# A fused three-layer kernel whose last layer transposes its softmax rows as fp32r, from copies made by DMA

## The chip, the cores and the metric

The kernel runs on one core of one Trainium2 chip. The metric is the device time of one execution in microseconds; smaller is better. The engines are TensorE (PE, with its weight loads shown apart as PEld), VectorE (DVE), ScalarE (ACT), GpSimd (POOL) and SyncE (SP), which here issues every DMA from one queue, in order.

## The reference, cut to what matters

Three layers follow each other on a batch of 8 sequences of 576 tokens and 512 channels: attention through 32 memory slots, a mixing layer over tokens and then channels, and a third layer that this case is about. That third layer runs four attention experts for every sequence, of which two count for a token:

```python
for e in range(E):                     # E = 4 experts, Hd = 64
    q = x @ wq[e]; k = x @ wk[e]; v = x @ wv[e]
    scores = scale * (q @ k.transpose(0, 2, 1))
    scores = np.where(causal, -1000000000.0, scores)
    scores = scores - scores.max(-1, keepdims=True)
    a = np.exp(scores)
    a /= a.sum(-1, keepdims=True) + 1e-09
    ye = a @ v @ wo[e]
    ...                                # out += gate weight * ye where e is among the two best
```

## The kernel before

The program has three stages on the same core: layer one with the token mixing (to about 310 us), the large channel matmuls in 512-token blocks (to about 737 us), and the last layer together with the rest of the channel mixing (from 737 us on). Only the third stage is touched. Matmul operands are kept as two fp32r parts, a high and a low one, so most products are three matmuls (`mm3`).

In the third stage a loop runs over `t` from 0 to 33; step `t` computes the scores of expert pass `t` (sequence `b = t // 4`, expert `e = t % 4`; below a pass is called n) and finishes pass `t - 1`. `scores` (line 1306) writes one 128-row block c of 128(c+1) columns: two matmuls, a mask and minimum on DVE, an exponential on ACT into `a`, one of two buffers of 1280 columns (blocks c = 0 to 3 side by side). The last 64 tokens of two experts share a block of their own: `tail_scores` into `atl`. `norm` (line 1344) works out the coefficient `cf` of each row (gate over row sum) on DVE, and scales: four multiplications on POOL for c = 0, 1, 2, 3 (line 1359), and every second pass one on ACT for `atl` (line 1355). In the next step `turn` (line 1361) transposes the scaled blocks on PE against `ident`, an fp32 identity, three 128x128 tiles for c = 2, three for c = 1 and four for c = 3 (line 1378), and splits the result out of PSUM into high and low parts for `weigh`, which multiplies them with v. `tail_turn` and line 1380 do the same with `atl`. Over the 32 passes that is 400 transposes.

Between these steps the loop fills in the channel mixing of the next sequence in halves j of 288 tokens: `load_2(j)` brings `u2[j]` (line 871, 576 KB), `split_2` makes its two parts `uh2` and `ul2` on POOL (lines 884 and 885), `mm1_2` and `mm2_2` multiply, and `mm2_2` adds to `p2[j]` (line 875) and splits the sum into `xh` and `xl` (line 1215). `u2` has two buffers, and `p2[1]` takes one of them too.

A program that lays out the kernel reorders the instructions of this stage by times of its own and fixes the order on each engine. So each engine runs a given list, and waits at an instruction until what it needs is there.

The four output matmuls of `project` end in `osb` tiles and DMAs to the output. For the last sequence, block c = 1, the two halves have tiles of their own (`oh0` and `oh1`, line 1462).

Of the kernel before, what the change touches and what calls it, by code (L numbers as in the profile page):

```python
# [9 lines left out]
F32 = mybir.dt.float32  # L10
# [15 lines left out]
def f(ap):  # L26
    return ap.bitcast(F32)
# [140 lines left out]
def fused_kernel(ctx: ExitStack, tc, q, k, v, phi, w_tok1, w_tok2, w_ch1, w_ch2,  # L168
# [693 lines left out]
        stg_ctx.close()  # L862


    c2 = None
    c2_ctx, w3_ctx = ExitStack(), ExitStack()
    u2, uh2, ul2, h2, p2 = {}, {}, {}, {}, {}

    def load_2(j):
        u2[j] = c2.tile([128, KD, SH], F32, name="u2", bufs=2)  # L870
        SP.dma_start(u2[j][:], u_d[:, SH * j:SH * j + SH].rearrange("(c p) s -> p c s", p=128))

    def load_p2(j):
        p2[j] = c2.tile([128, KD, SH], F32, name="u2", bufs=2) if j == 1 else c2.tile([128, KD, SH], F32, name="p2")
        SP.dma_start(p2[j][:], x_d[:, SH * j:SH * j + SH].rearrange("(c p) s -> p c s", p=128))

    def split_2(j, kd):
# [20 lines left out]
    with ExitStack() as sb:  # L898
# [189 lines left out]
        for i in range(NW + LAG):  # L1088
            items = [()] if i == NW else [work[i]] if work[i][0] in WIDE else [(*work[i], 0), (*work[i], 1)]
            for it in items:  # L1090
                if it:
# [10 lines left out]
                    for fc in fcs:  # L1102
                        if fc > N1 + 1:
                            next(prep, None)
                        if fc >= KM - KD:
                            load_p(n, fc - KM + KD)
                        if n == 0:
                            next(wcl, None)
                        if n == 1:
                            with tc.issue_after(latest(DVE)):  # L1110
                                for _ in range(2):
                                    next(sprep, None)
                        if n > WIDE[-1]:
                            for _ in range(7):
                                if next(wcl, 0) == 0 and c2 is None:
                                    stg_ctx.close()
                                    c2 = c2_ctx.enter_context(tc.tile_pool(name="c2", bufs=1, side="right"))
                                    load_2(0)
                                    load_2(1)
# [46 lines left out]
    with ExitStack() as sc:  # L1166
# [21 lines left out]
        smb = [wk_.tile([128, NQ], F32, name=f"sm{i}") for i in range(2)]  # L1188
        aoff = [0, 128, 384, 768]
        ab = [wk_.tile([128, 1280], F32, name=f"a{i}") for i in range(2)]  # L1190

        atl = wk_.tile([128, 640], F32, name="atl")
        POOL.memset(atl[:, S:640], 0.0)
# [150 lines left out]
        def norm(n):  # L1344

            b, e = divmod(n, E)
            w = NQ - e % 2
            cf = wk_.tile([128, NQ], F32, name="cf", bufs=2)
            DVE.tensor_scalar_add(cf[:, 0:w], smb[n % 2][:, 0:w], 1e-9)
            DVE.reciprocal(cf[:, 0:w], cf[:, 0:w])  # L1350
            DVE.tensor_mul(cf[:, 0:w], cf[:, 0:w], gt[b][:, e, 0:w])  # L1351
            a = ab[n % 2]
            for c in range(w):
                if c == NQ - 1:
                    ACT.activation(atl[:, 0:S], atl[:, 0:S], AF.Copy, scale=cf[:, c:c + 1])
                    continue
                W = 128 * c + 128
                x_ = a[:, aoff[c]:aoff[c] + W]
                POOL.tensor_mul(x_, x_, cf[:, c:c + 1].to_broadcast([128, W]))  # L1359

        def turn(n, c):

            e = n % 2
            a = ab[e]
            if n not in aA:
                aA[n] = (wk_.tile([128, 384], F32R, name="Ah"), wk_.tile([128, 384], F32R, name="Al"))
                if e == 0:
# [7 lines left out]
            p = pp.tile([128, 512], F32, name="t", bufs=2)  # L1375
            with tc.high_priority():
                for kc in range(k):
                    PE.transpose(p[:, 128 * kc:128 * kc + 128], a[:, o + 128 * kc:o + 128 * kc + 128], ident[:])  # L1378
                if c == 2 and e == 0:
                    PE.transpose(p[:, 384:512], atl[:, 512:640], ident[:])  # L1380
            if c == 1:
                split(Ah[:], Al[:], p[:, 0:384])
            else:
# [8 lines left out]
        def tail_turn(n):  # L1392

            Bh, Bl, Bt = aB[n // 2]
            p = pp.tile([128, 512], F32, name="t", bufs=2)
            with tc.high_priority():
                for kc in range(4):
                    PE.transpose(p[:, 128 * kc:128 * kc + 128], atl[:, 128 * kc:128 * kc + 128], ident[:])
            split(Bh[:, :, :, 256:320].rearrange("p e k q -> p k e q"), Bl[:, :, :, 256:320].rearrange("p e k q -> p k e q"),
                  p[:].rearrange("p (k e q) -> p k e q", k=4, e=2))  # L1400

        def weigh(n, part):
# [18 lines left out]
                ops.append((4, 256, Bt[:, e % 2, :]))  # L1421
            for i, (kc, lo, x) in enumerate(ops):
                PE.matmul(p[:, lo:w], lhsT=v_[:, kc, 0, :], rhs=x, start=(i == 0), stop=(i == len(ops) - 1))  # L1423
            t_ = wk_.tile([128, 320], F32, name="yb", bufs=2)
            ACT.activation(t_[0:64, 0:w], p[64:128, 0:w], AF.Copy)
            DVE.tensor_add(yt[o:o + 64, q0:q0 + w], p[0:64, 0:w], t_[0:64, 0:w])
            if e % 2:
# [24 lines left out]
        def project(b, c):  # L1452
            last = c == NQ - 1
            if last and b % 2 == 0:
                return
            cs = slice(0, 128) if last else slice(128 * c, 128 * c + 128)
            if b == B - 1 and c == 1:
                for i, w in enumerate((slice(0, 256), slice(256, 512))):
                    p = pp.tile([128, 512], F32, name="g", bufs=GB)[:, 0:256]
                    mm3(p, [((y[0][:, cs], y[1][:, cs]), (woh[:, pr, w], wol[:, pr, w]))  # L1460
                            for pr in range(2) for y in [yT[b, pr][1:]]], late="l")
                    o_ = late.tile([128, 256], F32, name=f"oh{i}")
                    if i:
                        DVE.tensor_copy(o_[:], p)
                    else:
                        ACT.activation(o_[:], p, AF.Copy)
                    SP.dma_start(out[b, cs, w], o_[:])
                return
            p = pp.tile([128, 512], F32, name="g", bufs=GB)
            mm3(p[:], [((y[0][:, cs], y[1][:, cs]), (woh[:, pr, :], wol[:, pr, :]))  # L1470
                       for pr in range(2) for y in [yE[b // 2, pr] if last else yT[b, pr][1:]]], late="l")
            o_ = late.tile([128, 512], F32, name="osb", bufs=2) if late else wk_.tile([128, 512], F32, name="osb", bufs=2)
            if b == B - 1 and c in (3, 0):
                DVE.tensor_copy(o_[:], p[:])
            else:
                ACT.activation(o_[:], p[:], AF.Copy)
            if last:
                SP.dma_start(out[b - 1, SM:S, :], o_[0:ST, :])
                SP.dma_start(out[b, SM:S, :], o_[ST:128, :])
            else:  # L1480
                SP.dma_start(out[b, cs, :], o_[:])
# [12 lines left out]
        for c in range(KD):  # L1494
            mm2_2(1, c)
        load_2(2)
        load_2(3)
        proj(0, 1, 1, 0, True)
        proj(0, 0, 1, 1, True)
        proj(0, 0, 0, 1, True)  # L1500
# [2 lines left out]
        for t in range(NE + 2):  # L1503
# [12 lines left out]
            if e == 0:  # L1516
# [6 lines left out]
                if b == B:  # L1523
                    held = [(project, B - 2, c) for c in range(4)]
            elif e == 1:
                if b < B:
                    fill = [(proj, b, 1, i, hf) for i, hf in KQ[2:4]]
                if 0 < b < B - 1 and b - 1 not in HELD:
                    fill += [(project, b - 1, c) for c in range(3)]
                if b == B - 1:  # L1530
# [3 lines left out]
            elif e == 2:  # L1534
# [7 lines left out]
                    fill += ([(mm2_2, 2 * b + 2, c) for c in range(KD)] + [(split_2, 2 * b + 3, kd) for kd in range(KD)] +  # L1542
                             [(mm1_2, 2 * b + 3, fc) for fc in PC] + [(load_p2, 2 * b + 3)])
                if b + 2 < B:
                    fill += [(load_2, 2 * b + 4), (load_2, 2 * b + 5)]
            elif e == 3 and not more:
                held = [(project, HELD[2], c) for c in range(1, 4)]
            elif e == 3 and more:
# [102 lines left out]
```

## Time and profile before

| what | value |
|---|---|
| median of 3 runs | 1213.23 us (1211.22 to 1215.14) |
| profiled execution | 1214.76 us, its span 1213.0 us |
| PE busy over the span | 96% |
| third stage, 737 us to the end | 476 us, PE busy 465.1 us |

The span runs from the first to the last instruction; 1.8 us of the execution's own time lie outside it. The profiled execution is 1.5 us above the median. Busy time of PE counts a matmul from its start to a modelled end, so that a busy PE is not a PE at its peak; the distance between the starts of two matmuls tells what one costs.

### The profile page before, as it was taken

Reading aid. Unit: us, or ns where it says so; the run is one execution under the profiler, and the core shown is the slowest. Engines: PE = TensorE matmul, PEld = TensorE weight load, DVE = VectorE, ACT = ScalarE, POOL = GpSimd, SP = SyncE. Lnnn points to the kernel's source line nnn. Section 1 sums busy time; section 2 is a strip of 40 time slices with the busy share of each in tenths; the row PEclk is TensorE's granted clock in tenths of the full one; section 3 lists DMA queues with packets and bytes.
Section 4 is the critical chain, followed back from the end, with each engine's and each line's share of the span. In section 5 each row is a group of like instructions: output and inputs, shape, how many; then the busy total and the mean of one; then the engine's idle time right before and its main releaser. Section 6 shows DMA issues by size and latency. Waiting matters only on the chain.

```text
span 1213.0 us, 23508 instructions
## 1 busy us (share of the span) xinstructions
PE 1165.3 (96%) x8586; PEld 1064.7 (88%) x8586; DVE 816.3 (67%) x1992; ACT 610.8 (50%) x1591; POOL 449.5 (37%) x603
## 2 busy tenths in 40 slices
PE   4899998999999999999999999999999999999998
PEld 3678887999888888889999889999999999999986
DVE  6999998665483756567566514777676767676664
ACT  3565565454442323223322213677676767677775
POOL 2774453442002012112111344545454627383331
PEclk9799999999999999999999999999999999999999
DMA  8896767532370221232123343322333333322522
GB/s 239 251 276 209 215 212 221 171 118 92 97 251 20 105 70 35 71 104 97 43 71 105 96 113 114 88 84 79 84 88 83 102 97 99 94 80 54 166 86 105
DMA packets 133780, 145.07 MB, mean 120 GB/s; under 512 B 35616, under 2 KB 101408, under 8 KB 133664
## 3 DMA queue, kind: packets, MB, share of 16 engines
q1 hardware_dynamic: 133664, 143.57, 39.2%
q8 instruction: 68, 1.11, 0.4%
q14 instruction: 48, 0.39, 0.1%
HBM read 91.10 MB, written 40.89 MB: 109 GB/s over the span
## 4 chain that ended last, share of the span: by engine, by line
PE 79%; DVE 11%; DMA 3%; issue 2%; ACT 2%; POOL 1%; SPq 0%; DVEq 0%; ACTq 0%; POOLq 0%
PE g L207 21%; PE o L207 16%; PE h L207 16%; PE y L1423 4%; PE b L207 3%; PE s L1314 3%; PE b L679 3%; PE t L1378 3%; PE s L1336 1%; DVE ul L670 1%; DVE cy L772 1%; PE g L623 1%; PE g L383 1%; PE g L624 1%; PE g L626 1%
## 5 line engine op out<-in xcount | busy, mean ns | idle before, releaser
L1359 POOL TENSOR_TENSOR a<-a,cf 128x128 f32<-128x128 f32 (+3 forms) x128 | 88.3, 723 | 68.9 <-DVE cf L1351 64.9
L207 PE MATMUL o<-hl,w2h 128*128 128x512 f32 x288 | 112.7, 391 | 0.3 <-DVE hl L931 0.3
L207 PE MATMUL o<-hh,w2l 128*128 128x512 f32 x288 | 112.3, 390 | 0.0
L207 PE MATMUL o<-hh,w2h 128*128 128x512 f32 x288 | 108.7, 392 | 0.2 <-DVE pb L1026 0.2
L930 ACT ACTIVATE hh<-m 128x256 fp32r<-128x256 f32 x96 | 38.9, 416 | 111.8 <-DVE m L1001 72.2
L1303 DVE CUSTOM_DVE_ANT_0 ssb<-s,cmask 128x128 f32<-128x128 f32 (+2 forms) x144 | 68.5, 483 | 27.3 <-PE s L1314 20.5
L1316 ACT ACTIVATE a<-ssb,nb 128x128 f32<-128x128 f32 (+3 forms) x128 | 71.3, 558 | 18.4 <-DVE nb L1303 15.1
L207 PE MATMUL h<-uh,w1h 128*128 128x512 f32 (+2 forms) x200 | 66.5, 334 | 4.7 <-ACT uh L211 4.7
L931 DVE SCALAR_TENSOR_TENSOR hl<-m,hh 128x256 fp32r<-128x256 f32 x96 | 58.2, 615 | 17.6 <-ACT hh L930 15.4
L978 POOL TENSOR_TENSOR tl<-ub,th 128x512 fp32r<-128x512 f32 x12 | 18.1, 1526 | 136.3 <-ACT th L977 136.3
L207 PE MATMUL h<-uh,w1l 128*128 128x512 f32 (+2 forms) x200 | 66.7, 334 | 0.0
L1215 POOL TENSOR_TENSOR xl<-p,xh 128x288 fp32r<-128x288 f32 x60 | 47.4, 811 | 51.8 <-ACT xh L1214 51.6
L207 PE MATMUL h<-ul,w1h 128*128 128x512 f32 (+2 forms) x200 | 66.1, 335 | 0.0
L207 PE MATMUL g<-xh,qkh 128*128 128x288 f32 x232 | 65.3, 301 | 0.0
L207 PEld LDWEIGHTS o<-hh,w2l 128*128 128x128 f32 x288 | 54.1, 188 | 11.3
L207 PE MATMUL g<-xh,qkl 128*128 128x288 f32 x232 | 63.9, 296 | 0.0
L207 PEld LDWEIGHTS o<-hh,w2h 128*128 128x128 f32 x288 | 54.0, 188 | 10.7 <-DVE pb L1026 1.0
L963 POOL TENSOR_TENSOR ub<-ub 128x512 f32<-128x512 f32 x6 | 9.8, 1628 | 144.4 <-DVE ul L214 144.4
L207 PEld LDWEIGHTS o<-hl,w2h 128*128 128x128 f32 x288 | 54.1, 188 | 10.0 <-DVE hl L931 0.6
L214 DVE TENSOR_TENSOR Bl<-t,Bh 128x512 fp32r<-128x512 f32 (+1 forms) x80 | 50.5, 633 | 14.3 <-ACT Bh L211 12.6
L923 DVE SCALAR_TENSOR_TENSOR hl<-h,hh 128x512 fp32r<-128x512 f32 x24 | 16.5, 689 | 59.9 <-ACT hh L922 59.8
L1430 POOL TENSOR_TENSOR yl<-yt,yh 128x256 fp32r<-128x256 f32 x30 | 22.2, 739 | 85.0 <-ACT yh L1429 74.9
(340 smaller groups left out, 4123.8 us busy)
## 6 DMA issues: line engine op xcount, KB each, us to landing
cst<-in_moe_w_ch_dram SPq DMA_DIRECT2D x24, 512.0 KB, 4.8
u_d<-u SPq DMA_DIRECT2D x32, 288.0 KB, 3.6
p_d<-u SPq DMA_DIRECT2D x16, 576.0 KB, 4.2
ub<-u_d SPq DMA_DIRECT2D x9, 1024.0 KB, 5.7
pb<-p_d SPq DMA_DIRECT2D x36, 256.0 KB, 4.1
x_d<-pb SPq DMA_DIRECT2D x36, 256.0 KB, 2.1
u<-u_d SPq DMA_DIRECT2D x16, 576.0 KB, 4.2
p<-x_d SPq DMA_DIRECT2D x15, 576.0 KB, 4.1
```

The source lines that it names most:

```text
L207: PE.matmul(ps, lhsT=a, rhs=b, start=start and i == 0, stop=stop and i == len(seq) - 1)
L214: DVE.tensor_sub(lo, src, f(hi))
L679: PE.matmul(h1[j, fc, "p"][:], lhsT=w[:, kd, :], rhs=x[:, kd, :], start=(part == 0 and i == 0), stop=(part == 1 and i == KD - 1))
L930: ACT.activation(hh, c, AF.Relu)
L931: DVE.scalar_tensor_tensor(hl, c, 0.0, f(hh), op0=OP.max, op1=OP.subtract)
L1215: POOL.tensor_sub(xl[b][:, c, ss], x_, f(xh[b][:, c, ss]))
L1303: DVE.tensor_tensor_reduce(out=out, in0=p, in1=mask, scale=-scale, scalar=least, op0=OP.add, op1=OP.min, accum_out=acc)
L1314: PE.matmul(p[:, 0:W], lhsT=q_[n][:, 128 * c:128 * c + 128], rhs=kk[n][:, 0:W], start=(i == 0), stop=(i == 1))
L1316: ACT.activation(a[:, aoff[c]:aoff[c] + W], s_[:, 0:W], AF.Exp, scale=-1.0, bias=nb[:, 0:1], accum_out=sm[:, c:c + 1])
L1359: POOL.tensor_mul(x_, x_, cf[:, c:c + 1].to_broadcast([128, W]))
L1378: PE.transpose(p[:, 128 * kc:128 * kc + 128], a[:, o + 128 * kc:o + 128 * kc + 128], ident[:])
L1423: PE.matmul(p[:, lo:w], lhsT=v_[:, kc, 0, :], rhs=x, start=(i == 0), stop=(i == len(ops) - 1))
```

## The change

For 31 of the 32 passes (all but the last) the scaled softmax rows are no longer transposed from `a` itself. SP copies them by DMA into `ar`, a tile of the same size that is typed fp32r, and PE transposes that against an fp32r identity `identr`, which ACT makes once. The copies are three for each pass (c = 2; c = 0 and 1 together; c = 3), and POOL multiplies in that order. The tail rows `atl` are copied to `atr` in all 16 cases. `ar` and `atr` have one buffer each. The copies add 31 x 3 + 16 = 109 DMAs, and about 25 MB, to SP's queue. To make room, `u2` goes down to one buffer (half 1 alone has a place of its own), `yb` goes down to one buffer, and the last output tiles share `osb`; `load_2` of an odd half is called three steps later than before.

```diff
     def load_2(j):
-        u2[j] = c2.tile([128, KD, SH], F32, name="u2", bufs=2)
+        u2[j] = (wk8 if j == 1 else c2).tile([128, KD, SH], F32, name="u2")
...
     def load_p2(j):
-        p2[j] = c2.tile([128, KD, SH], F32, name="u2", bufs=2) if j == 1 else c2.tile([128, KD, SH], F32, name="p2")
+        p2[j] = c2.tile([128, KD, SH], F32, name="u2" if j == 1 else "p2")
...
+        identr = wk_.tile([128, 128], F32R, name="identr")
+        ACT.activation(identr[:], ident[:], AF.Copy)
+        ar = {}
...
             a = ab[n % 2]
-            for c in range(w):
-                if c == NQ - 1:
-                    ACT.activation(atl[:, 0:S], atl[:, 0:S], AF.Copy, scale=cf[:, c:c + 1])
-                    continue
-                W = 128 * c + 128
-                x_ = a[:, aoff[c]:aoff[c] + W]
-                POOL.tensor_mul(x_, x_, cf[:, c:c + 1].to_broadcast([128, W]))
+            copied = n < NE - 1
+            ar[n] = wk_.tile([128, 1280], F32R, name="ar") if copied else a
+            if e % 2 == 0:
+                ar["t"] = wk_.tile([128, 640], F32R, name="atr")
+                ACT.activation(atl[:, 0:S], atl[:, 0:S], AF.Copy, scale=cf[:, NQ - 1:NQ])
+            for cs in ((2,), (0, 1), (3,)):
+                for c in cs:
+                    W = 128 * c + 128
+                    x_ = a[:, aoff[c]:aoff[c] + W]
+                    POOL.tensor_mul(x_, x_, cf[:, c:c + 1].to_broadcast([128, W]))
+                if copied:
+                    o = slice(aoff[cs[0]], aoff[cs[-1]] + 128 * cs[-1] + 128)
+                    SP.dma_start(f(ar[n][:, o]), a[:, o])
+                if e % 2 == 0 and cs == (2,):
+                    SP.dma_start(f(ar["t"][:]), atl[:])
...
-            a = ab[e]
+            a = ar[n]
+            idn, ty = (identr, F32R) if n < NE - 1 else (ident, F32)
...
-                    PE.transpose(p[:, 128 * kc:128 * kc + 128], a[:, o + 128 * kc:o + 128 * kc + 128], ident[:])
+                    PE.transpose(p[:, 128 * kc:128 * kc + 128].bitcast(ty), a[:, o + 128 * kc:o + 128 * kc + 128], idn[:])
...
-            t_ = wk_.tile([128, 320], F32, name="yb", bufs=2)
+            t_ = wk_.tile([128, 320], F32, name="yb")
...
             if b == B - 1 and c == 1:
+                o2 = wk_.tile([128, 512], F32, name="osb", bufs=2)
...
-                    o_ = late.tile([128, 256], F32, name=f"oh{i}")
+                    o_ = o2[:, w]
...
         load_2(2)
-        load_2(3)
...
             elif e == 1:
+                if more:
+                    fill += [(load_2, 2 * b + 3)]
...
-                    fill += [(load_2, 2 * b + 4), (load_2, 2 * b + 5)]
+                    fill += [(load_2, 2 * b + 4)]
```

The order on the engines shows three places. The first is PE where pass 28 is transposed (`t` is the PSUM tile, `s` the scores of pass 29, `g` an output projection). Before:

```order
L207 MATMUL g<-woh,yl_14879 128x512
L1314 MATMUL s<-kk,qa 128x512
L1314 MATMUL s<-kk,qb 128x512
L207 MATMUL g<-woh,yl_14883 128x512
L1378 MATMUL t<-ident,a_8610 128x128 x6
L1380 MATMUL t<-ident,atl 128x128
L207 MATMUL g<-woh,yh_14878 128x512
```

And in the change, from the same scores to the last of the same seven transposes:

```order
L1319 MATMUL s<-kk,qa 128x512
L1319 MATMUL s<-kk,qb 128x512
L1392 MATMUL t<-identr,ar 128x128 x3
L207 MATMUL g<-woh,yh_15024 128x512
...
L207 MATMUL g<-woh,yl_15029 128x512
L1394 MATMUL t<-identr,atr 128x128
L1392 MATMUL t<-identr,ar 128x128 x3
```

What stood in one run of seven is now a run of three and a run of four, with 12 projection matmuls between. Between the last tail score of pass 28 and its first transpose there were 87 matmuls with 28,064 columns, and there are now 73 with 24,696. Over the whole stage the 400 transposes stood in 93 unbroken runs, so that 307 were followed at once by another; they now stand in 107 runs, and of the 390 fp32r ones 286 are followed at once by another.

The second place is SP's queue at the start of the third stage (names that begin with `u_` are buffers of `u2` and, on line 875, of `p2[1]`). Before, `u_8774` is half 2:

```order
L1027 DMA x_d<-pb 128x512 x4
L871 DMA u_8774<-u_d 128x4x288
L875 DMA p_9208<-x_d 128x4x288
L871 DMA u_8776<-u_d 128x4x288
L871 DMA u_9381<-u_d 128x4x288
L1245 DMA qb<-qa 64x576
```

In the change half 2 is `u_8780`:

```order
L1027 DMA x_d<-pb 128x512 x4
L875 DMA p_9224<-x_d 128x4x288
L871 DMA u_8780<-u_d 128x4x288
L1250 DMA qb<-qa 64x576
L1249 DMA qa<-qb 64x576
```

The load of half 2 stood first and could go as soon as half 1 had been split; it now goes into the buffer that `p2[1]` holds, and so behind the last reader of `p2[1]`. On PE, 36 projection matmuls of 288 columns (into three tiles) now stand between the end of `mm2_2(1)` and the first matmul that reads half 2, where there were none.

The third place is the end of ACT's list, the last output tiles. Before:

```order
L1425 ACTIVATE yb<-y 64x256
L1429 ACTIVATE yh<-yt 128x256
L1476 ACTIVATE osb<-g 128x512 x2
L1466 ACTIVATE oh_15742<-g 128x256
L1646 UNCONDITIONAL_BRANCH
```

And in the change:

```order
L1439 ACTIVATE yb<-y 64x256
L1443 ACTIVATE yh<-yt 128x256
L1491 ACTIVATE osb<-g 128x512 x2
L1481 ACTIVATE osb<-g 128x256
L1662 UNCONDITIONAL_BRANCH
```

The order is the same; the last half tile is now a buffer of `osb`, which the tail block (c = 4) filled two tiles earlier.

## Rows read from the trace of the kernel before

**Rows 1.** The page's first part: busy time, share of the span and instructions.

```profile
PE 1165.3 (96%) x8586; PEld 1064.7 (88%) x8586; DVE 816.3 (67%) x1992; ACT 610.8 (50%) x1591; POOL 449.5 (37%) x603
```

**Rows 2.** Third stage: us, busy PE, PEld, DVE, ACT, POOL, granted clock, DMA share, GB/s.

```profile
737.00:1213.00 476.00, 465.12 (x3396) 447.95 (x3396) 320.13 (x1028) 329.48 (x952) 230.21 (x354) 1.00 0.33 95
```

**Rows 3.** Groups by form, 737 us to the end: busy us, mean ns.

```profile
L1378 PE MATMUL t<-ident,a 128*128 128x128 f32 x320 | 48.8, 274 | 0.1
```

**Rows 4.** Timeline of PE, transposes of pass 28: start us, us from first start to last end.

```profile
1167.50 0.82 PE L1378 MATMUL t<-ident,a 128*128 128x128 f32 x6
1168.16 0.27 PE L1380 MATMUL t<-ident,atl 128*128 128x128 f32 x1
...
1168.50 0.39 PE L207 MATMUL g<-wol,yh 128*128 128x512 f32 x1
```

**Rows 5.** Timeline of PE, two 128-column fp32r matmuls in a row.

```profile
981.71 0.22 PE L1314 MATMUL s<-kk,qa 128*128 128x128 f32 x1
981.76 0.28 PE L1314 MATMUL s<-kk,qb 128*128 128x128 f32 x1
981.88 0.33 PE L1314 MATMUL s<-kk,qa 128*128 128x256 f32 x1
```

**Rows 6.** Plain fp32 weight loads of 128 columns (line 393), ns min/median/max.

```profile
L393 PEld LDWEIGHTS g<-ones,es x28: 186/190/338, 38.5 to 272.3; 128*128 128x128 f32 x28
```

**Rows 7.** Plain fp32 matmuls of 128 columns (line 383), ns min/median/max.

```profile
L383 PE MATMUL g<-kv,ea x640: 270/273/423, 9.9 to 271.6; 128*32 128x128 f32 x160
```

**Rows 8.** Line 439, transposes with 128 weight and 32 moving columns.

```profile
L439 PEld LDWEIGHTS t<-ident,qe x64: 132/138/221, 14.6 to 279.2; 32*128 32x128 f32 x64
L439 PE MATMUL t<-ident,qe x64: 221/222/311, 14.6 to 279.2; 32*128 32x32 f32 x64
```

**Rows 9.** Timeline of PE, four of these.

```profile
187.74 0.43 PE L439 MATMUL t<-ident,qe 32*128 32x32 f32 x4
```

**Rows 10.** POOL's scaling by form, 737 us to the end.

```profile
L1359 POOL TENSOR_TENSOR a<-a,cf 128x384 f32<-128x384 f32 x32 | 26.6, 830 | 0.0
...
L1359 POOL TENSOR_TENSOR a<-a,cf 128x256 f32<-128x256 f32 x32 | 19.7, 616 | 0.0
...
L1359 POOL TENSOR_TENSOR a<-a,cf 128x128 f32<-128x128 f32 x32 | 12.9, 402 | 68.9 <-DVE cf L1351 64.9 <-ACT Bh L211 3.3
```

**Rows 11.** Timeline, pass 28: after its last tail score, and its scaling on POOL.

```profile
1154.30 0.28 PE L207 MATMUL g<-vgh,xh 128*128 128x260 f32 x1
...
1163.80 2.76 POOL L1359 TENSOR_TENSOR a<-a,cf 128x128 f32<-128x128 f32 x4 [0.61 <-DVE cf L1351]
```

**Rows 12.** DMA issues: count, KB each, median us from issue to landing.

```profile
qb<-qa SPq DMA_DIRECT2D x32, 144.0 KB, 2.4
...
yh<-y_d SPq DMA_DIRECT2D x6, 256.0 KB, 5.1
...
out_dram<-osb SPq DMA_DIRECT2D x8, 128.0 KB, 2.4
```

**Rows 13.** Timeline, start of the third stage.

```profile
747.91 0.29 PE L207 MATMUL g<-uh,w1h 128*128 128x288 f32 x1
...
748.34 0.82 DVE L1213 TENSOR_TENSOR u<-u,g 128x288 f32<-128x288 f32 x2
...
749.88 1.59 POOL L1215 TENSOR_TENSOR xl<-u,xh 128x288 fp32r<-128x288 f32 x2
...
751.50 1.12 SPq L871 DMA_DIRECT2D u<-u_d  x2
...
755.53 1.55 POOL L884 CAST uh<-u 128x288 fp32r<-128x288 f32 x4 [3.30 <-DMA u<-u_d]
```

**Rows 14.** Timeline, the end.

```profile
1208.08 0.59 SPq L1479 DMA_DIRECT2D out_dram<-osb  x1
1208.55 0.42 DVE L1464 COPY oh<-g 128x256 f32<-128x256 f32 x1
...
1209.39 0.89 SPq L1467 DMA_DIRECT2D out_dram<-oh  x2
```

More of the change, by code (lines that the diff above doesn't have):

```diff
@@ L862, in fused_kernel @@
         stg_ctx.close()
-    c2 = None
+    c2 = wk8 = None
     c2_ctx, w3_ctx = ExitStack(), ExitStack()
@@ L1116, in fused_kernel @@
                                     stg_ctx.close()
+                                    wk8 = sb.enter_context(tc.tile_pool(name="wk8", bufs=1))
                                     c2 = c2_ctx.enter_context(tc.tile_pool(name="c2", bufs=1, side="right"))
@@ L1377, in turn @@
                 for kc in range(k):
-                    PE.transpose(p[:, 128 * kc:128 * kc + 128], a[:, o + 128 * kc:o + 128 * kc + 128], ident[:])
+                    PE.transpose(p[:, 128 * kc:128 * kc + 128].bitcast(ty), a[:, o + 128 * kc:o + 128 * kc + 128], idn[:])
                 if c == 2 and e == 0:
-                    PE.transpose(p[:, 384:512], atl[:, 512:640], ident[:])
+                    PE.transpose(p[:, 384:512].bitcast(F32R), ar["t"][:, 512:640], identr[:])
             if c == 1:
@@ L1397, in tail_turn @@
                 for kc in range(4):
-                    PE.transpose(p[:, 128 * kc:128 * kc + 128], atl[:, 128 * kc:128 * kc + 128], ident[:])
+                    PE.transpose(p[:, 128 * kc:128 * kc + 128].bitcast(F32R), ar["t"][:, 128 * kc:128 * kc + 128], identr[:])
             split(Bh[:, :, :, 256:320].rearrange("p e k q -> p k e q"), Bl[:, :, :, 256:320].rearrange("p e k q -> p k e q"),
@@ L1461, in project @@
                             for pr in range(2) for y in [yT[b, pr][1:]]], late="l")
-                    o_ = late.tile([128, 256], F32, name=f"oh{i}")
+                    o_ = o2[:, w]
                     if i:
-                        DVE.tensor_copy(o_[:], p)
+                        DVE.tensor_copy(o_, p)
                     else:
-                        ACT.activation(o_[:], p, AF.Copy)
-                    SP.dma_start(out[b, cs, w], o_[:])
+                        ACT.activation(o_, p, AF.Copy)
+                    SP.dma_start(out[b, cs, w], o_)
                 return
@@ L1471, in project @@
                        for pr in range(2) for y in [yE[b // 2, pr] if last else yT[b, pr][1:]]], late="l")
-            o_ = late.tile([128, 512], F32, name="osb", bufs=2) if late else wk_.tile([128, 512], F32, name="osb", bufs=2)
+            o_ = wk_.tile([128, 512], F32, name="osb", bufs=2)
             if b == B - 1 and c in (3, 0):
@@ L1525, in fused_kernel @@
             elif e == 1:
+                if more:
+                    fill += [(load_2, 2 * b + 3)]
                 if b < B:
-                    fill = [(proj, b, 1, i, hf) for i, hf in KQ[2:4]]
+                    fill += [(proj, b, 1, i, hf) for i, hf in KQ[2:4]]
                 if 0 < b < B - 1 and b - 1 not in HELD:
```

## The prediction, written before the result was known

> **What bounds the kernel now.** I read the page's first part for the engine that is nearest to full: PE, 96% of the span [rows 1]. Then the stretch in which the change lies: in the 476 us of the third stage PE is busy 465.1 us, ACT 329, DVE 320 and POOL 230, the granted clock is 1.00 (the 2.4 GHz level) and the DMA engines are busy a third of the time [rows 2]. So the third stage is a list of PE instructions with some 11 us of gaps in 476. Whatever shortens that list shortens the kernel, as long as the others keep up; whatever makes PE wait at a point of the list lengthens it by the wait. Everything below is one or the other.
>
> **What a transpose costs now.** A group of the view by form gives 274 ns for one [rows 3], but that is a duration with its pipeline in it. The timeline gives the spacing: six transposes last 0.82 us from first start to last end, so (0.82 - 0.27) / 5 = 0.110 us lie between two starts [rows 4]; I use 109 ns, as 1168.16 - 1167.50 = 0.66 is six of them. The last of a run is followed by a plain matmul: from 1168.16 to the second matmul behind it, at 1168.50, go 0.34 us. A column of plain work costs 13.20 us / 28,064 = 0.47 ns (both numbers under 2, below), so the 512-column matmul between takes 0.24 and the last transpose 0.10 to 0.11 too.
>
> **What an fp32r transpose would cost.** No row of before shows one, so I bound it. It is a weight load of 128 columns (the softmax tile) and a pass of 128 columns (the identity).
> The pass: a plain fp32 matmul of 128 columns lasts 273 ns [rows 7], as the fp32 transpose does, while a plain fp32r one of 128 columns lasts 0.22 us and the next may start 0.05 to 0.06 us later [rows 5]. So the length of the pass goes by the type, and an fp32r pass should be spaced by about 59 ns.
> The load: a plain fp32 load of 128 columns lasts 190 ns [rows 6], a transpose's 138 ns [rows 8]: here the mode counts. Four transposes with 128 weight columns and only 32 moving ones last 0.43 us, (0.43 - 0.222) / 3 = 0.069 us apart [rows 8, 9], so loads in this mode can follow each other every 69 ns at most.
> Against this stands the plain fp32r load. Of the two 128-column matmuls in [rows 5] the second starts 0.05 us after the first, but what follows it starts 0.12 us after that: 0.17 us for the two, where two passes would take 0.12. The second waited for its weights, which came about 0.11 us after the first began. If an fp32r transpose loads like that, it is spaced by 111 ns and nothing is gained.
> I take 64 ns, between 59 and 69, because two rows say that the mode sets the load and the type the pass. The bounds are 59 and 111.
> One page of the Trainium skill speaks against it: "TensorE: Matmul & The Clock Gate", section "LDWEIGHTS (loading the stationary operand)", gives a load of P columns as P / 1.2 ns, 107 ns for 128, whatever else it is; by it the sum below would hold 286 x 2 ns = 0.6 us of gain instead of 12.9. The plain pair [rows 5] agrees with it, the four short transposes [rows 9] do not, and the rows decide.
>
> **The sum.** (1) In a run of transposes only those that are followed by another get shorter, since the last one pays for the plain load behind it (0.11 us, as above). The order of the change has 286 fp32r ones followed by another: 286 x (109 - 64) = **-12.9 us**. Bounds: 286 x 50 = -14.3, and 286 x 2 = +0.6.
>
> (2) The copies. A block's way from POOL to PE gets longer by a DMA. The nearest row is the SBUF-to-SBUF copy `qb<-qa`, 2.4 us from issue to landing [rows 12]; 2.0 is thinkable, and 5.1 as the upper end, the slowest of that size class. POOL now scales c = 2 first, which saves 0.402 + 0.616 = 1.02 us [rows 10]. So the first transpose of a pass may come 1.4 us later than now without loss. I took the distance from POOL's end to the first transpose for each pass, and corrected it by the PE work that the new order puts between the last score and that transpose. Most passes have 1.5 to 10 us left. The worst is pass 28. There PE went from 1154.30 to 1167.50, 13.20 us, through 28,064 columns [rows 4, 11]; the new order has 24,696, so 13.20 x 24,696 / 28,064 = 11.6 us, and PE is at its transpose at 1165.9. POOL started at 1163.80, so c = 2 is scaled at 1164.63 [rows 10, 11] and copied at 1167.0: PE waits **+1.1 us**, and behind it the pass's other matmuls. Three other passes with e = 0 or 2 come out within 0.6 us of nothing left; I charge **+0.5 us**. Bounds for both together: 0 and, with 4 us for a copy, about 10.
> SP pays about 0.5 us for each of 109 issues, spread over the stage, and waits in the order in which POOL works; at nothing, and if it queues, the copies come later, which is the bound just given. POOL does the same work in another order; ACT gets one activation more. `yb` with one buffer: the DVE add that frees it comes before the next ACT write in all 64 cases of the trace; at nothing.
>
> (3) `u2` with one buffer. In the steady part the next load can go when POOL has split the half before, some 10 us or more ahead of its use, and takes 4 us; hidden. If that cover were gone, it would cost up to 4 us for each of 15 halves. At the start it is not hidden. Half 2 now waits for the last reader of `p2[1]`, which is `xl` on POOL. The DVE adds end at 749.16 [rows 13], ACT's copy and POOL's subtraction (0.81 each at most) behind them, without the split that now stands between them on POOL, bring that to about 750.4. Issue to the first cast took 755.53 - 751.50 = 4.0 us [rows 13], the cast takes 0.4: half 2 is ready at 754.8. PE ended `mm2_2(1)` at 747.91 and now has 36 projections of 288 columns before it needs it, 36 x 288 x 0.47 ns = 4.9 us, at 752.8. PE waits **+2.0 us**. Bounds: 0 if other waits have made PE late by then, 3.2 if the reader is as late as now (load at 751.50).
>
> (4) The end. The last half tiles write into the `osb` buffer that the tail block filled, and so wait for its two DMAs. The second is issued at 1208.08 and lands 2.4 us later [rows 12, 14], at 1210.5; a copy out of PSUM takes 0.42 us [rows 14], so the first of the two last DMAs is issued at 1210.9 instead of 1209.39: **+1.5 us**. Bounds 1.0 and 2.0. Nothing is behind it to hide it.
>
> Together -12.9 + 1.1 + 0.5 + 2.0 + 1.5 = -7.8 us. The profiled execution took 1214.8 us, so it becomes 1207.0; it lies 1.5 us above the median, and against that I forecast **1205.4 us**.
>
> **The rivals.** *The fp32r transpose costs what the fp32 one does* (slower). Its place is the weight load: if an fp32r tile loads like the plain fp32r weights of [rows 5], the spacing is 111 ns, term 1 is +0.6 and the others stay: 1213.2 + 5.7 = 1218.9 us. It decides above 109 - 5.1 / 0.286 = 91 ns, where the gain no longer pays for the waits. For it speaks that plain loads do that in every type; against it the loads of [rows 8, 9]. The page of the Trainium skill cited above would have it so. 17%.
>
> *The copies come late in many passes.* For it: one queue carries everything, 109 DMAs more, and `yh<-y_d` needed 5.1 us when twelve were sent together [rows 12]. At 4.1 us for a copy the margins of nine passes are gone and the waits add up to some 8.5 us more: about 1214 us, no change. Against it: DMA engines are busy 0.33 [rows 2], and 25 MB more at the stage's rate bring that to about half. 12%.
>
> *The waits are smaller than I make them*, because PE arrives late for other reasons, and the transposes reach 59 ns: -14.3 + 1.5 gives 1200.4 us. Little speaks against it except the arithmetic of (2) and (3). 8%.
>
> The forecast itself has 63%, with 1202 to 1209 as its own range.
>
> **How the numbers follow.** About 0.3% is what a measurement of this kernel tells from no change: below 1209.6 is faster, above 1216.9 slower. The forecast and the third rival are faster but for a tail (0.69); the first rival is slower; the second divides between no change and slower. So 0.69, 0.13 and 0.18. The range runs from 1200 to 1218.5: it leaves out the lower half of the third rival, the upper half of the first, and copies slower than 4.5 us.
>
> **What would show it.** A run of three fp32r transposes should last about 0.22 + 2 x 0.064 = 0.35 us from first start to last end, and one's weight load 138 ns; with 0.44 us and 188 ns the first rival is right. PE's busy time in the third stage should fall from 465 to about 452. The waits of PE should name the DMA `ar<-a` at pass 28 for about 1 us and at few other places, and once, near 753, the cast of half 2 for about 2 us. At the end ACT's last copy should stand idle for a DMA of `osb`. The forecast is wrong if the transposes keep their spacing, or if waits for `ar` come back in most passes with e = 0.

## The result: slower, 1227.7 us

The change takes 1227.68 us (median of 4 runs, 1225.24 to 1228.20) against 1213.28 us before (4 runs): a ratio of 1.0115 with an interval of 1.0094 to 1.0137, or 14.4 us more where 7.8 us less was forecast.

The first part of the page and the row of the third stage answer to [rows 1, 2]:

```profile
PE 1165.0 (95%) x8586; PEld 1057.2 (86%) x8586; DVE 820.4 (67%) x1992; ACT 609.8 (50%) x1592; POOL 450.3 (37%) x603
```

```profile
737.00:1227.00 490.00, 466.61 (x3405) 442.80 (x3403) 325.31 (x1031) 329.25 (x952) 229.09 (x353) 1.00 0.46 144
```

PE is busy about as long as before, though its transposes got cheaper (below), and the stage is longer; the granted clock is 1.00 in both, the DMA share went from 0.33 to 0.46. So a gain was made and more than given back. Where, is seen in what each queue waits for. Each row names the instruction that waits, what it waits for, and how long: us in total, times, longest. First PE in the third stage, then SP (SPq is its DMA queue):

```profile
PE t L1392 <- DMA ar<-a: 3.1, 5, 1.5
PE t L207 <- DVE kk L1241: 2.0, 2, 1.6
PE s L1319 <- DVE nb L1308: 1.9, 5, 0.6
PE g L207 <- DVE p L1218: 1.5, 2, 0.9
PE y L1437 <- ACT Bh L211: 1.5, 2, 1.0
```

```profile
SPq L1250 <- ACT qa L1243: 68.1, 13, 15.6
SPq L1370 <- PE t L1392: 47.4, 13, 6.5
...
SPq L1370 <- POOL a L1367: 11.7, 21, 2.4
```

No single wait of PE is large. But SP stands 47 us, in 13 places, before a copy into `ar` (line 1370) because PE has not finished the transposes of the pass before; with all other releasers it stands 105 us before the copies of lines 1370 and 1372. These are not yet costs. Before, SP stood even longer in the third stage, about 385 us in all its waits against about 340 in the change, the largest of them being

```profile
SPq L1245 <- ACT qa L1238: 83.6, 13, 16.1
SPq L871 <- POOL ul L885: 56.4, 11, 11.5
```

SP is not short of time; it matters at which instruction of its list it stands, and what PE needs from behind it.

The view of waits counts only time in which no matmul is running by its modelled end, and so undercounts. I therefore took the starts of all PE matmuls in the third stage of each trace. A plain matmul is priced at the median distance to the next start for its column count (0.060 us for 128, 0.120 for 256 and 260, 0.133 for 288, 0.148 for 320, 0.175 for 384, 0.232 for 512), transposes at the mean distance between two in a run (leaving out the few distances that hold a wait), and the end of a run at its median. The end of a run is the time from its last transpose to the second matmul behind it, less the first one's own price. What is left is waiting; by how the medians are taken it moves by about 1 us. In us, with the experiments below:

| kernel | transpose to transpose | end of a run | transposes together | waits | last matmul to end of span |
|---|---|---|---|---|---|
| before | 307 x 0.109 | 93 x 0.112 | 43.9 | 19.5 | 4.8 |
| the change | 293 x 0.074 | 107 x 0.155 | 38.2 | 35.9 | 5.9 |
| e1, no copies, fp32 | 295 x 0.110 | 105 x 0.112 | 44.1 | 20.9 | 6.0 |
| e2, copies, fp32 | 288 x 0.110 | 112 x 0.112 | 44.1 | 36.0 | 6.1 |
| e3, no copies, fp32r | 282 x 0.073 | 118 x 0.153 | 38.6 | 19.6 | 6.3 |
| e4, three tiles, fp32r | 291 x 0.073 | 109 x 0.156 | 38.0 | 31.5 | 6.1 |
| e5, unread copies, fp32 | 297 x 0.110 | 103 x 0.112 | 44.1 | 28.4 | 5.9 |
| e7, before with fp32r | 310 x 0.076 | 90 x 0.157 | 37.8 | 19.1 | 4.8 |

The plain matmuls come to 407 to 410 us in all of these. Of the 19.5 us of waits before, the view of waits shows 6; the other 13 are scatter around the medians and the 0.1 to 0.2 us by which each wait is undercounted, and something like them is in every row. The change: -5.7 (transposes) + 16.4 (waits) + 1.2 (plain) + 1.1 (end) = +13.0 of the 13.2 us by which the span grew. No plain matmul got dearer: in the change seven more of them lie behind 737 us.

### The profile page after: what moved, and what is told of

Read it like the earlier page. It is cut to its first block, busy times and chain, and to the rows that moved or that the text cites. A ratio compares the mean times of both kernels' runs of the same rounds, so it can differ in the third digit from the quotient of the medians.

```text
span 1226.2 us, 23676 instructions
## 1 busy us (share of the span) xinstructions
PE 1165.0 (95%) x8586; PEld 1057.2 (86%) x8586; DVE 820.4 (67%) x1992; ACT 609.8 (50%) x1592; POOL 450.3 (37%) x603
## 4 chain that ended last, share of the span: by engine, by line
PE 72%; DVE 12%; DMA 7%; ACT 4%; issue 2%; POOL 2%; SPq 1%; DVEq 0%; ACTq 0%; POOLq 0%
PE g L207 18%; PE o L207 16%; PE h L207 15%; PE b L207 3%; PE y L1437 3%; PE b L679 3%; PE s L1319 2%; PE t L1392 1%; DMA qn<-in_q_dram 1%; DMA p<-x_d 1%; POOL a L1367 1%; PE g L623 1%; PE s L1341 1%; DVE ul L670 1%; PE g L624 1%
## 5 line engine op out<-in xcount | busy, mean ns | idle before, releaser
L1367 POOL TENSOR_TENSOR a<-a,cf 128x256 f32<-128x256 f32 (+3 forms) x128 | 88.0, 720 | 67.5 <-DVE cf L1356 55.3
L214 DVE TENSOR_TENSOR Bl<-t,Bh 128x512 fp32r<-128x512 f32 (+1 forms) x80 | 50.4, 633 | 19.5 <-ACT Bh L211 17.1
L207 PEld LDWEIGHTS o<-hl,w2h 128*128 128x128 f32 x288 | 54.1, 188 | 10.3 <-DVE hl L931 0.7
```

The source lines that it names most:

```text
L207: PE.matmul(ps, lhsT=a, rhs=b, start=start and i == 0, stop=stop and i == len(seq) - 1)
L214: DVE.tensor_sub(lo, src, f(hi))
```

## The experiments

Ratios are to the kernel before, measured beside each experiment (12.1 us is 1%), with their 95% intervals.

**e1, the change without its copies and without fp32r.**

```diff
-            copied = n < NE - 1
+            copied = False
...
-                ar["t"] = wk_.tile([128, 640], F32R, name="atr")
+                ar["t"] = atl
...
-                if e % 2 == 0 and cs == (2,):
-                    SP.dma_start(f(ar["t"][:]), atl[:])
...
-            idn, ty = (identr, F32R) if n < NE - 1 else (ident, F32)
+            idn, ty = ident, F32
...
```

> The change without its copies and without fp32r: the transposes read the softmax rows themselves, against the fp32 identity; one u2 buffer, one yb buffer, the shared osb and POOL's new order stay. In the trace of the change PE's waits are 18 us longer than before, and the transposes and what follows them 7.6 us shorter. Theory A (the copies make the waits: their time, SP's queue, the one buffer of ar): only the start and the end remain, some 2.4 + 1.1 us, so 1215 to 1219 us. Theory B (the smaller buffers and the new order of PE make them): the waits stay and the gain is gone, 1230 us or more.

Measured 1215.46 us, 1.0029 (1.0017 to 1.0040): 3.4 us. The smaller buffers and the new order cost no more than the start and the end. Theory B is out: the copies make the waits, directly or through the order that is laid out around them, since every kernel here has an order of its own.

**e2, the change with fp32 copies and transposes**, the tail's too.

```diff
-            ar[n] = wk_.tile([128, 1280], F32R, name="ar") if copied else a
+            ar[n] = wk_.tile([128, 1280], F32, name="ar") if copied else a
...
-            idn, ty = (identr, F32R) if n < NE - 1 else (ident, F32)
+            idn, ty = ident, F32
...
```

> The change with ar and atr typed fp32 and transposed against the fp32 identity: the copies stay, the cheaper transposes go. If the type of the transposes is worth what the trace of the change shows (293 transposes that are followed by another at 67 instead of 109 ns, less 106 times 43 ns for the plain matmul that follows a run, so 7.6 us), and all else stays: 1227.7 + 7.6 = 1235 us. If the shorter transposes only make PE wait longer for the same copies, the type is worth nothing and it stays at 1226 to 1230 us.

Measured 1230.44 us, 1.0145 (1.0128 to 1.0162). It lies between the two expectations, at the upper edge of the second. Against the change, by the two ratios, that is 0.3% (3.6 us) for the type, and the intervals overlap; the table gives 5.9 us for the transposes and equal waits. Against e1 the copies cost 1.16%, 14 us.

**e3, the change without copies, with fp32r transposes.** POOL and ACT write the rounded rows themselves.

```diff
...
-                    POOL.tensor_mul(x_, x_, cf[:, c:c + 1].to_broadcast([128, W]))
-                if copied:
-                    o = slice(aoff[cs[0]], aoff[cs[-1]] + 128 * cs[-1] + 128)
-                    SP.dma_start(f(ar[n][:, o]), a[:, o])
+                    POOL.tensor_mul(ar[n][:, aoff[c]:aoff[c] + W], x_, cf[:, c:c + 1].to_broadcast([128, W]))
```

> The change without its copies, but with fp32r transposes: POOL and ACT write the scaled rows straight into ar and atr, rounded to fp32r, so the low part of the rows is lost. One u2 buffer, one yb buffer and the shared osb stay. Theory A (the copies make the waits): the run before of this call less 7.6 us, 1207 to 1212 us. Theory B (buffers and order make them): 1222 to 1228 us, as the change.

Measured 1210.82 us, 0.9995 (0.9981 to 1.0008), inside theory A's interval. Against e1 the type is worth 0.34%, 4 us, where the table has 5.5; the waits are those of e1, 19.6 and 20.9. The copies of the change move the rows bit for bit; here they are rounded and lose their low part, as in e7, e8 and e11.

**e4, three tiles for ar.**

```diff
...
-                    SP.dma_start(f(ar[n][:, o]), a[:, o])
+                    ar[n, cs[-1]] = wk_.tile([128, o.stop - o.start], F32R, name=f"ar{cs[-1]}")
+                    SP.dma_start(f(ar[n, cs[-1]][:]), a[:, o])
...
```

> The change with three tiles (384, 384 and 512 columns) in place of the one tile ar of 1280, so that the copy of a block waits only for the transposes of that block one pass earlier, not for all ten. In the trace of the change SP waits 47 us in 13 places for the transposes before it can issue such a copy. Theory A1 (that wait, and what stands behind it on SP, makes the waits of PE): 1214 to 1219 us. Theory A2 (the time of a copy, 2.4 us, between POOL and PE makes them) or B: 1224 to 1229 us.

Measured 1220.11 us, 1.0062 (1.0050 to 1.0074), between the two expectations. The one tile costs about 0.5%, 6 us, and its interval does not meet the change's; 8 us over e3 remain (9 by the two medians).

How the one tile holds the copies up shows in the trace of the change (start us, us from first start to last end; in brackets how long the engine had stood, and for what):

```profile
833.71 5.46 POOL L1367 TENSOR_TENSOR a<-a,cf 128x384 f32<-128x384 f32 x8 [8.57 <-DVE cf L1356]
...
838.99 0.40 ACT L1321 ACTIVATE a<-ssb,nb 128x128 f32<-128x128 f32 x1 [3.66 <-DMA ar<-a]
...
843.32 0.45 PE L1392 MATMUL t<-identr,ar 128*128 128x128 f32 x4
843.85 2.31 SPq L1370 DMA_DIRECT2D ar<-a  x3
```

POOL had scaled two passes by 839.2. The three copies of the second go out at 843.85, after the last four transposes of the first (843.77), though the first blocks of `ar` had long been read. A copy holds its source too: shortly before, ACT, which must not overwrite `a` before a copy has read it, had stood for 3.66 us until a copy of the first pass had landed.

**e5, copies that nobody reads.** The kernel of e1, with copies in the three tiles of e4:

```diff
+                if n < NE - 1:
+                    o = slice(aoff[cs[0]], aoff[cs[-1]] + 128 * cs[-1] + 128)
+                    un = wk_.tile([128, o.stop - o.start], F32R, name=f"ar{cs[-1]}")
+                    SP.dma_start(f(un[:]), a[:, o])
+                if e % 2 == 0 and cs == (2,):
+                    ut = wk_.tile([128, 640], F32R, name="atr")
+                    SP.dma_start(f(ut[:]), atl[:])
```

> The kernel of e1 (fp32 transposes of the softmax rows themselves, small buffers) with the 109 copies added in three tiles and one for the tail, which nobody reads. So the copies load SP's queue and the DMA engines and hold the buffers a and atl, but are not in the way from POOL to PE. The three tiles of e4 cost 9.3 us over e3, which has no copies. Theory A3 (SP's queue: what stands behind a copy that waits for POOL comes late): most of the 9 us come back, 1221 to 1226 us. Theory A2 (the time of a copy between POOL and PE): as e1, 1214 to 1218 us.

Measured 1223.17 us, 1.0088 (1.0074 to 1.0101): 7 us over e1, as much as the read ones of e4 cost over e3 (8 us). So that PE must wait for a copy's 2.4 us (theory A2) is a matter of 1 or 2 us, about what these intervals tell; by the starts of the matmuls PE waits 1.4 us right before transposes of `ar` in e4. SP's queue in e5:

```profile
SPq L1371 <- POOL a L1367: 32.8, 43, 4.6
SPq L1450 <- ACT yeh L1457: 27.6, 3, 16.7
SPq L1374 <- ACT a L1321: 18.6, 3, 8.0
```

Lines 1371 and 1374 are the unread copies: SP still stands 84 us before them with all releasers, and all that is behind them stands too. But the copies also hold `a` and `atl`, so e5 does not show that the queue alone makes the 7 us.

**e6, e4 with the copies issued by POOL and ACT.**

```diff
-                    SP.dma_start(f(ar[n, cs[-1]][:]), a[:, o])
+                    POOL.dma_start(f(ar[n, cs[-1]][:]), a[:, o])
...
-                    SP.dma_start(f(ar["t"][:]), atl[:])
+                    ACT.dma_start(f(ar["t"][:]), atl[:])
```

> The kernel of e4 (three tiles, copies read as fp32r) with the copies of the rows issued by POOL and those of the tail by ACT, each behind its own scaling, so that SP's queue is as it was before. Theory A3 (SP's queue): near e3, 1210 to 1214 us. Theory A2 (the time of a copy): it stays near e4, 1218 to 1222 us, or is longer, since POOL now waits for the transposes of the pass before.

Measured 1259.42 us, 1.0388 (1.0374 to 1.0402). This did not test SP's queue, since it made POOL a worse one. Two groups of POOL in the third stage (busy us, mean ns, idle before and its releasers):

```profile
L1367 POOL TENSOR_TENSOR a<-a,cf 128x384 f32<-128x384 f32 (+3 forms) x128 | 87.9, 717 | 26.6 <-DVE cf L1356 24.5 <-ACT qa L1243 1.5
L1371 POOL DMA_DIRECT2D ar<-a x93 | 51.7, 557 | 46.2 <-issue 14.9 <-PE t L1397 9.9 <-PE t L1395 7.1
```

Each issue takes 0.56 us of POOL, 52 us together, and 46 us go in waits in front of them, for transposes among others, while the splits of `u2` and `p2` stand behind on POOL. The Trainium skill, "DMA: Bandwidth & Descriptors", section "Issuing engines are not separate DMA queues", says that issuing from several engines only saves the sequencer's time of issue; here that time was moved onto an engine that had work to do.

**e7, the kernel before with the type alone.** The exponentials and the scaled rows are written, rounded, as fp32r into `a` and `atl`:

```diff
-        ab = [wk_.tile([128, 1280], F32, name=f"a{i}") for i in range(2)]
+        ab = [wk_.tile([128, 1280], F32R, name=f"a{i}") for i in range(2)]
+        identr = wk_.tile([128, 128], F32R, name="identr")
+        ACT.activation(identr[:], ident[:], AF.Copy)
...
-                POOL.tensor_mul(x_, x_, cf[:, c:c + 1].to_broadcast([128, W]))
+                POOL.tensor_mul(x_, f(x_), cf[:, c:c + 1].to_broadcast([128, W]))
...
```

> The kernel before with nothing but the type of the transposes changed: the exponentials and the scaled rows are written as fp32r into the same tiles a and atl (rounded), and transposed against identr. No copies, no second tile, all buffers as before. The transposes and what follows them are worth 7.7 us by the traces (43.9 us before, 36.2 to 36.4 us with fp32r in three kernels); the start (2.4 us) and the end (1.2 us) of e3 go away too. By that sum 1204 to 1206 us. If the shorter list of PE only waits more elsewhere, 1208 to 1211 us.

Measured 1206.16 us, 0.9952 (0.9938 to 0.9967): 5.8 us faster, at the upper edge of the sum. The table's 43.9 - 37.8 = 6.1 us is that gain; the 7.7 of the expectation (and the 7.6 of e1 to e3) had taken 67 ns, the median, for the distance of two transposes, where the mean is 74 to 76.

**e8, e7 without the low parts**, which are zero there, since the rows are already rounded:

```diff
...
-                split(Bh[:, e, 0:k, q0:q0 + 128], Bl[:, e, 0:k, q0:q0 + 128],
-                      p[:, 0:128 * k].rearrange("p (k q) -> p k q", k=k))
+                ACT.activation(Bh[:, e, 0:k, q0:q0 + 128], p[:, 0:128 * k].rearrange("p (k q) -> p k q", k=k), AF.Copy)
...
-                ops = [(kc, 128 * kc, x[:, 256 * kc:256 + 128 * kc]) for x in (Ah, Al) for kc in range(2)]
+                ops = [(kc, 128 * kc, x[:, 256 * kc:256 + 128 * kc]) for x in (Ah,) for kc in range(2)]
...
```

> The kernel of e7 without the low parts Al and Bl of the transposed rows, which are zero there since the rows are already rounded to fp32r: six matmuls fewer in each of the 32 passes (two for Ah's columns, four for Bh's, of 128 to 320 columns), and three subtractions fewer on DVE. If PE is the bound there: 2 x (256 + 128) / 2 and 3 x 320 + 192 columns make 1536 columns a pass, at 0.47 ns a column 0.72 us, for 32 passes 23 us below e7, about 1182 us. If ACT or DVE or POOL bound it by then, 5 to 15 us.

Measured 1184.38 us, 0.9771 (0.9758 to 0.9785): 28 us faster than before, 22 us faster than e7. PE's busy time in the third stage falls to 434 of 445 us, and it is still the engine that bounds:

```profile
737.00:1182.40 445.40, 433.78 (x3187) 414.88 (x3186) 261.05 (x911) 323.22 (x948) 226.91 (x350) 0.99 0.34 99
```

**e9 and e10, what about an unread copy costs.** Both are e5 but for what is copied, the tail's copy likewise. e9 copies 16 columns each, behind the same waits; e10 copies whole blocks of `kk`, which is ready early.

```diff
-                    SP.dma_start(f(un[:]), a[:, o])
+                    SP.dma_start(f(un[:, 0:16]), a[:, o.stop - 16:o.stop])
...
```

```diff
-                    SP.dma_start(f(un[:]), a[:, o])
+                    SP.dma_start(f(un[:]), f(kk[n][:, 0:o.stop - o.start]))
...
```

> The kernel of e5 with its 109 unread copies at the same places of SP's queue, behind the same waits for POOL, but of 16 columns each (8 KB instead of 192 to 320 KB). e5 cost 7 us over e1. Theory A4 (SP's queue: copies that wait for POOL hold up what stands behind them): it stays near e5, 1220 to 1225 us. Theory A5 (the bytes: the other transfers get slower while the copies run): as e1, 1214 to 1217 us.

> The kernel of e5 with its 109 unread copies at nearly full size (192 and 256 KB, 288 KB for the tail), but taken from the keys kk, which are ready early, so that the copies wait for neither POOL nor ACT. Theory A4 (the waits for POOL in SP's queue): as e1, 1214 to 1217 us. Theory A5 (the bytes): near e5, 1220 to 1225 us.

Measured 1220.58 us, 1.0072 (1.0061 to 1.0084), and 1219.82 us, 1.0060 (1.0047 to 1.0073). Over e1 that is 5 us and 4 us, where e5 has 7 us. Taking away nearly all bytes leaves most of the cost, as theory A4 has it; the intervals of e9 and e5 overlap. But taking away the waits for POOL and ACT (SP stands 28 us before the copies instead of 84, and 18 of these 28 for an earlier copy into the same tile) leaves half, which A4 has not. So the waits for POOL and ACT do not make the 7 us alone, and the bytes are not shown to have a part; see below.

**e11, e7 with each transpose of the rows twice.**

```diff
-                    PE.transpose(p[:, 128 * kc:128 * kc + 128].bitcast(F32R), a[:, o + 128 * kc:o + 128 * kc + 128], identr[:])
+                    for _ in range(2):
+                        PE.transpose(p[:, 128 * kc:128 * kc + 128].bitcast(F32R), a[:, o + 128 * kc:o + 128 * kc + 128], identr[:])
```

> The kernel of e7 with each of the 320 transposes of the rows a issued twice in a row (the tail's 80 once), so that the runs get longer and the result stays. By the traces an fp32r transpose starts 60 and 65 ns behind the first two of a run, and 85 ns behind the later ones. If a weight load every 85 ns sets the pace once the loads ahead are used up: 320 x 85 ns = 27 us more than e7, 1233 us. If the pass of 60 ns set it and the 85 are waits of another kind: 19 us more, 1225 us. If each cost the 109 ns of fp32: 35 us more, 1241 us.

Measured 1231.81 us, 1.0158 (1.0145 to 1.0172). Against e7 that is 2.07%, 25 us, 78 ns for each of the 320: nearest to the pace of 85 ns, not to 60 or 109. By the starts of the matmuls the transposes take 64.8 us instead of 37.8, 84 ns for each of the 320.

## Why the prediction was wrong, point by point

The step that failed is in (2): it put the waits of SP for the copies "at nothing", and so the copies at 1.6 us, where they cost some 15. Term (1) went the right way, but was taken at more than twice its size.

**(1) The transposes, forecast -12.9 us, measured -5.7.** The direction held, the first rival (111 ns, no gain) is out. A run of three in the change with its weight loads:

```profile
785.22 0.35 PEld L1392 LDWEIGHTS t<-identr,ar 128*128 128x128 f32 x3
785.35 0.37 PE L1392 MATMUL t<-identr,ar 128*128 128x128 f32 x3
785.52 0.30 PEld L207 LDWEIGHTS g<-hl,w2h 128*128 128x128 f32 x2
785.56 0.50 PE L207 MATMUL g<-hl,w2h 128*128 128x288 f32 x2
...
785.89 0.29 PE L207 MATMUL g<-hh,w2h 128*128 128x288 f32 x1
```

Two things were mis-sized. The step "I take 64 ns" holds for the second and third of a run only: by position the distances are 60, 65, and then 85 ns. So the mean is 74 and not 64 ns, 293 x 35 ns = 10.3 us. And the step "the last one pays for the plain load behind it (0.11 us, as above)" took the end of a run from the fp32 rows [rows 4]. There the load of the next plain weights starts together with the last transpose:

```profile
1168.16 0.27 PE L1380 MATMUL t<-ident,atl 128*128 128x128 f32 x1
1168.16 0.19 PEld L207 LDWEIGHTS g<-woh,yh 128*128 128x128 f32 x1
```

Here it starts at 785.52, but the last transpose at 785.35 + 0.37 - 0.24 = 785.48 (0.24 is the mean duration in the group by form): the pass has become shorter than the loads, the loads run behind, and the plain one waits its turn. Over all 107 ends of a run, that load starts 49 ns behind the last transpose's start at the median; in the 93 before it was 2 ns. From the last transpose to the second matmul behind it less that first matmul's own time, 0.155 us go instead of 0.112, 107 x 43 ns = 4.6 us. -10.3 + 4.6 = -5.7. PE's busy time, which I expected to fall from 465 to about 452 us, does not show this gain: it is 466.6 in the change, with the short waits that this count hides, and 460.1 in e7. The rule of the Trainium skill that spoke against the gain ("TensorE: Matmul & The Clock Gate", section "LDWEIGHTS (loading the stationary operand)", 107 ns for 128 columns) is contradicted by 85 ns, the pace of a long run (e11). The same page's section "Back-to-back issue gap" gives about 81 ns for a stream of load and matmul pairs of 128 columns, and with that the 85 agree.

**(2) The copies, forecast +1.6 us with bounds 0 and 10, measured some 15.** This is the step that turned the sign. The waits are 35.9 us with copies and 19.6 without (e3), 36.0 and 20.9 with fp32 (e2, e1). I followed the path of a block from POOL to PE and asked whether a copy of 2.4 us fits into its margin. That was right as far as it went: copies land in 2.3 us (192 KB) and 2.5 us (256 KB) at the median, and PE waits for one 3.1 us in all. The longest, 1.5 us, was at pass 27, one before the one I named, and comes with twelve loads of `y_d` around it, as the second rival had it. The three copies of that pass needed 6.5 to 8.5 us to land, more than the 5.1 us that the rival took its case from, at a DMA share of 0.95 and more from 1144.9 to 1153.5 us:

```profile
1143.47 0.59 SPq L1463 DMA_DIRECT2D yh<-y_d  x1
...
1144.96 3.67 SPq L1370 DMA_DIRECT2D ar<-a  x3
...
1153.53 0.45 PE L1392 MATMUL t<-identr,ar 128*128 128x128 f32 x3 [1.47 <-DMA ar<-a]
```

What I did not follow is who waits at the copy. "SP ... waits in the order in which POOL works; at nothing" was the wrong step. By the starts of the matmuls, the waits of more than 0.12 us grew from 8.3 to 23.4 us, and only 3.8 us of that stand before the transposes that read `ar`. The rest stands before the products with v (4.4, line 1437), the scores (2.6), the channel mixing and the projections (1.9), and at the start (2.3, see (3)): PE was held up by what came late elsewhere. First, `ar` is one tile with one buffer, so a copy for the first block waits for PE's last transposes of the pass before: 47 us of SP, worth 6 us of time (the change against e4). Second, copies that nobody reads cost 7 us (e5 against e1). SP takes its list in order, so `qa`, `qb`, `qz`, `u2`, `p2` and the output stand behind each wait for a copy, and each copy holds `a`; which of the two it is, is not shown. The second rival looked at the right place, but it too counted only PE's waits for `ar`: 1.6 + 8.5 = 10 us.

What the 7 us of the unread copies are made of stays open. Fewer bytes (e9) and fewer waits (e10) each leave 4 to 5 us, so the presence of 109 more issues, the buffers that they hold and the order that is laid out anew around them may all have a part. No run puts the copies into an order that is otherwise unchanged. The orders differ in all these kernels, and differences of 2 us between them can't be given to one cause.

**(3) The start, forecast +2.0 us: the size was right by luck, the wait another.** In the change, and alike in e1 to e3:

```profile
750.87 0.37 PE L207 MATMUL t<-xh,qkh 128*128 128x288 f32 x1 [1.61 <-DVE kk L1241]
...
754.69 0.37 PE L207 MATMUL t<-xh,qkh 128*128 128x288 f32 x1 [0.41 <-DVE kk L1241]
...
755.60 1.54 POOL L884 CAST uh<-u 128x288 fp32r<-128x288 f32 x4 [4.20 <-DMA u<-u_d]
```

PE stood 2.0 us, but not for half 2, whose cast began at 755.60 (I had it done by 754.8). The 36 projections that now stand in a row write tiles `t` of PSUM (the memory of PE's results), of which there are two, and wait for DVE to empty them. These waits gave half 2 the time it needed. In e7, with the buffers of before, neither is there.

**(4) The end, forecast +1.5 us, measured +1.1.** From the last matmul's start to the end of the span go 5.9 us instead of 4.8. The copy into the shared `osb` waits for its DMAs:

```profile
1220.82 0.54 SPq L1496 DMA_DIRECT2D out_dram<-osb  x1
1222.71 0.38 ACT L1481 ACTIVATE osb<-g 128x256 f32<-128x256 f32 x1 [3.16 <-DMA out_dram<-osb]
1222.92 0.42 DVE L1479 COPY osb<-g 128x256 f32<-128x256 f32 x1 [2.23 <-DMA out_dram<-osb]
1223.12 0.81 SPq L1482 DMA_DIRECT2D out_dram<-osb  x2
```

So all four terms have the right sign and three are within their bounds, and the one that was called almost free is larger than all the others. `yb` and `u2` in the steady part cost nothing that e1 would show.

## What to carry to other kernels

A copy put between a producer and PE has three prices, and the time of the transfer is the smallest here: ask also who must have read the target before it may be written (split the target by reader: 6 us here), and what the copy holds up by merely being there, on the queue that issues it and in the buffer that it reads (7 us here, not taken apart). On an engine that is 96% full, price an instruction by the distance between starts, separately for the inside and the end of a run, because a shorter instruction hands part of its gain to the load behind it. And where only a type is wanted and the rounding can be borne, let the producer write that type: here it gave 5.8 us without a copy or a buffer, and made the work on the low parts needless, another 22 us.

## What the runs showed of the hardware that was not expected

At a granted clock of 1.00, an fp32r transpose of 128 x 128 starts 60, 65, 85, 85 ... ns behind the one before it (the change, e11), an fp32 one 109 ns at every place of a run (before); its weight load lasts 140 ns in both. The plain matmuls behind an fp32r run come 43 ns later than behind an fp32 run. A copy of 8 KB needs 1.8 us from issue to landing and one of 192 KB 2.4 us at the median (e9, e5), so an SBUF-to-SBUF copy's time here hardly depends on its size. It depends on what else is under way: behind nine loads of 256 KB, one of 192 KB took 8.5 us (the change, 1144.96 us).
